# First attention tile with one Newton step for all heads, weights converted one slot ahead of use, and earlier weight splits

## The chip, the cores and the metric

The kernel runs on one NeuronCore of a Trainium2 chip. The engines that matter are TensorE (PE, matrix products), VectorE (DVE), ScalarE (ACT), GpSimd (POOL) and SyncE (SP, which issues most transfers). The metric is the device time of one execution in microseconds, as the median of the runs shown. A profile comes from one of those executions, with times counted from its first instruction.

## The reference

Linear attention of 8 batches, 8 heads, 576 positions and head width 64, with a normalisation, then a two-layer network with a rational activation on 4608 tokens (512 to 2048 to 512), all in float32:

```python
kv = np.einsum('bhsd,bhse->bhde', k, v)
out = np.einsum('bhsd,bhde->bhse', q, kv)
rms = np.sqrt(np.mean(out * out, axis=-1, keepdims=True) + 1e-06)
x = out / rms * g_norm   # heads side by side: 4608 x 512
h = x @ w_in
P = a[0] + a[1] * h + a[2] * h**2 + a[3] * h**3
Q = 1.0 + np.abs(b[0]) * np.abs(h) + np.abs(b[1]) * h**2
out = (P / (Q + 1e-06)) @ w_out
```

The two weight matrices arrive as 64-bit floats; their bits are passed in as 64-bit integers and turned into float32 on the chip.

## The kernel before, in words

**Tiles and slots.** The 4608 tokens are nine tiles of 512. The hidden width is 16 chunks of 128. The work runs in 9 x 16 slots (t, c): a slot takes the product of the first layer for one chunk (`gemm1`, h), the activation (`ew_a` to `ew_d`: L423 to L447 on ScalarE and VectorE, giving g), and the second layer's product (`gemm2`) into four accumulators. In slot i, TensorE's order is gemm2 of slot i - 2, a piece of the attention of the next tile, then gemm1 of slot i + 1 (in the first four slots gemm1 stands ahead of the attention). The order of each engine's queue is the order of the code from L569 on; nothing is rearranged there. h has two buffers.

**Precision.** A tile after the first splits every float32 operand into a high and a low part of the type fp32r and takes three products (low by high, high by low, high by high: L413 to L415, L474 to L476). In the first tile the weights are used whole, in one float32 product (L409, L470), since they aren't split yet.

**Weights.** They come as 16 units, eight of `wi` and eight of `wo`, each of two chunks. A unit is fetched by SyncE (`fetch_w`, L156, 1 MB), then its two 32-bit words are scaled on ScalarE (`conv_a`, L172), put together on VectorE (`conv_b`, L189, L194, L195), and later split (`split_w`): a copy to fp32r (L216), and the difference from it on VectorE (L223). The table `schedule` (L120) gives for each unit the slots in which it is fetched, scaled, put together and split, which engine takes what (S for ScalarE, G for GpSimd), and where in the slot the two halves of `conv_b` stand. In this version each split stands in the slot before the unit's first use in tile 1, the copy of the `wo` units is GpSimd's, and units are put together two to three slots ahead of use in tile 0, except the last ones.

**Attention.** For tile t + 1 it is spread over the slots of tile t: K·V of a pair of heads (`att_kv`, L297) in even slots, the product with q (`att_o`) in odd ones, then the mean squares of all heads in one accumulator (`att_ms`), one reciprocal root by ScalarE's Ln and Exp with a Newton step on VectorE (`newton_rstd`, L246 to L252), a spread of that row over partitions through DRAM, and the normalisation (`att_norm`, L376). For tile 1 both are whole float32 products, and the K·V copies stand in `split_kv` (L234, L240, L241).

**The first tile's attention** (L529 to L578) has nothing to hide behind. It takes K·V, o, squares, mean squares, Newton step and normalisation one pair at a time: the mean squares are taken with a matrix `own` that gives every partition its own head's mean at once, so that each pair has its own Ln, Exp, Square (L246 to L248), its own two Newton operations (L251, L252) and its normalisation (L565). Between them stand the two halves of the first unit's conversion ("a0 b0 a1 b1" in `order`, L575).

Of the kernel before, what the change touches and what calls it, by code (L numbers as in the profile page):

```python
# [23 lines left out]
def linear_attention_then_rational_ffn(  # L24
# [51 lines left out]

    ZSC = 2.0**-40
# [25 lines left out]
    zero = work.tile([P, P], F32, tag="at", name="zero", bufs=4)  # L103
    POOL.memset(zero, 0.0)
    for i in range(NKV):
        DVE.tensor_copy(kvh[i], zero)
        DVE.tensor_copy(kvl[i], zero)


    kvf = wpool.tile([P, 2, NPAIR, P], F32, tag=f"f{NF - 1}", name="kvf")  # L110
    POOL.memset(kvf, 0.0)

    def f32(t):
# [5 lines left out]

    schedule = {  # L120
# [16 lines left out]
    }  # L137
    units = list(schedule)
# [11 lines left out]
    def fetch_w(u):  # L150
        kind, c = u
        k = units.index(u) % NG
        raws[u] = wpool.tile([P, 2 * DM], I64, tag=f"g{k}", name=f"raw_{kind}{c}")
        src = w_in[c:c + 2].rearrange("c p k f -> p c (k f)") if kind == "wi" else \
            w_out[c:c + 2].rearrange("c p f -> p c f")
        nc.sync.dma_start(raws[u].rearrange("p (c f) -> p c f", c=2), src)  # L156
# [9 lines left out]
    both = slice(0, 2 * DM)  # L166
# [7 lines left out]
    copy = {"S": ACT.copy, "V": DVE.tensor_copy, "G": POOL.tensor_copy}  # L174

    def conv_a(u, part=both):
        low, high = words(u, part)
        engines = schedule[u][4]
        scale(engines[0], f32(high), f32(high), 2.0**-112)
        scale(engines[1], low, low.bitcast(U32), 2.0**-29)  # L180
# [25 lines left out]
    def split_w(u):  # L206
# [9 lines left out]
        copy[schedule[u][4][2]](wh, w)  # L216
# [220 lines left out]
    def ew_c(t, c, fill=lambda k: None):  # L437
# [5 lines left out]
        if t == 0:  # L443
# [17 lines left out]
    def gemm2(t, c, subs=range(NSUB)):  # L461
# [4 lines left out]
        for k, s in enumerate(subs):  # L466
            ss = slice(k * P, (k + 1) * P)
            o = acc[t][s]
            if t == 0:
# [59 lines left out]
    o0, ms0 = {}, {}  # L529

    def first_kv(p):
        ps = ps_at.tile([P, TW], F32, tag=("at", "ms")[p % 2], name=f"kvp_0_{p}", bufs=1)
# [25 lines left out]
    def first_rstd(p):
        r0[p] = work.tile([P, TW], F32, tag="d", name=f"r_0_{p}")
        r2 = work.tile([P, TW], F32, tag="u", name=f"r2_0_{p}")  # L560
        todo[p] = newton_rstd(ms0[p], r0[p], r2)

    def first_norm(p):
        todo[p]()
        DVE.scalar_tensor_tensor(x0[:, p], o0[p], ghalf, r0[p], ALU.mult, ALU.mult)  # L565

    x0 = xpool.tile([P, NPAIR, TW], F32, tag="xB", name="x0")
    warm = ps_h.tile([P, TW], F32, tag="h", name="warm")
    ctx.enter_context(tc.manual_schedule())  # L569
    PE.matmul(warm, own, kvf[:, 1].rearrange("p a b -> p (a b)"), start=True, stop=True)  # L570
    POOL.tensor_scalar(ghalf, gcol, -0.5, None, ALU.mult)
    steps = {"k": first_kv, "o": first_o, "s": first_sq, "m": first_ms, "r": first_rstd, "x": first_norm,
             "a": lambda n: conv_a(units[0], slice(n * DM, (n + 1) * DM)),
             "b": lambda n: conv_b(units[0], slice(n * DM, (n + 1) * DM))}
    order = "k0 k1 o0 o1 s0 m0 k2 k3 s1 m1 o2 o3 r0 r1 " \  # L575
            "x0 s2 s3 a0 m2 x1 b0 a1 b1 m3 r2 r3 x2 x3"
    for step in order.split():
        steps[step[0]](int(step[1]))  # L578
    for u in at_slot(0, -1)[:3]:
        fetch_w(u)  # L580
    fetch_kvq(1, 0)
    for u in at_slot(0, -1)[3:]:
        fetch_w(u)


    for k in (-2, -1):
        for u in at_slot(2, k):
            conv_b(u)
        for u in at_slot(1, k):
            conv_a(u)  # L590
# [76 lines left out]
```

## Time and profile before

| what | value |
|---|---|
| median of three runs | 948.72 us (948.35 to 952.35) |
| profiled execution, its own time | 952.35 us |
| its span, first to last instruction | 950.5 us |
| TensorE busy | 906.5 us, 95% |
| VectorE busy | 814.2 us, 86% |
| ScalarE busy | 684.8 us, 72% |
| GpSimd busy | 13.8 us, 1% |
| moved by the transfers | 63.78 MB |
| mean granted TensorE clock | 0.983 |

A busy share is an average over stages with different limits, and products are pipelined, so that a busy TensorE isn't one at its peak. The profile's views that are shown later: a table of stretches (busy time of each engine in each, the granted clock, the share of the transfer engines and what they moved), the waits (who waited for whom, in total, how often, the longest), groups of instructions by line, and the timeline (start, duration, engine, line, output<-inputs, shapes, and in brackets the idle time before it and what ended that). A line number is that of the code that issued the instruction; line 172 is the scaling helper, line 234 the copy of K·V.

### The profile page before, as it was taken

Reading aid. Unit: us, or ns where it says so; the run is one execution under the profiler, and the core shown is the slowest. Engines: PE = TensorE matmul, PEld = TensorE weight load, DVE = VectorE, ACT = ScalarE, POOL = GpSimd, SP = SyncE. Lnnn points to the kernel's source line nnn. Section 1 sums busy time; section 2 is a strip of 40 time slices with the busy share of each in tenths; the row PEclk is TensorE's granted clock in tenths of the full one; section 3 lists DMA queues with packets and bytes.
Section 4 is the critical chain, followed back from the end, with each engine's and each line's share of the span. In section 5 each row is a group of like instructions: output and inputs, shape, how many; then the busy total and the mean of one; then the engine's idle time right before and its main releaser. Section 6 shows DMA issues by size and latency. Waiting matters only on the chain.

```text
span 950.5 us, 11596 instructions
## 1 busy us (share of the span) xinstructions
PE 906.5 (95%) x4234; PEld 682.3 (72%) x4234; DVE 814.2 (86%) x1275; ACT 684.8 (72%) x1154; POOL 13.8 (1%) x26
## 2 busy tenths in 40 slices
PE   6599997999979999999999999999999999999998
PEld 3244433776758878887888788878887888788886
DVE  4989998798976789878987898879877998898887
ACT  4867765767656777877786778677877697777766
POOL 1000111000000000000000000000000000000000
PEclk9999998999979999999999999999999999999999
DMA  8634400310103210321032113101310110101001
GB/s 318 243 139 188 167 23 1 116 61 12 45 0 117 73 37 9 117 72 33 14 117 66 28 25 117 61 23 35 106 48 12 45 55 23 33 14 45 1 0 45
DMA packets 26935, 63.78 MB, mean 67 GB/s; under 512 B 3264, under 2 KB 5312, under 8 KB 26880
## 3 DMA queue, kind: packets, MB, share of 16 engines
q1 hardware_dynamic: 26432, 63.06, 20.2%
q8 instruction: 33, 0.54, 0.2%
q14 instruction: 22, 0.18, 0.1%
q10 hardware_dynamic: 448, 0.00, 0.0%
HBM read 53.48 MB, written 9.57 MB: 66 GB/s over the span
## 4 chain that ended last, share of the span: by engine, by line
PE 77%; DVE 16%; ACT 4%; issue 2%; DMA 1%; SPq 0%; DVEq 0%; ACTq 0%
PE h L413 12%; PE acc L475 12%; PE acc L476 11%; PE h L414 11%; PE h L415 11%; PE acc L474 11%; PE kvp L297 2%; PE acc L470 2%; DVE u L441 2%; DVE q L425 2%; DVE u L433 1%; DVE q L439 1%; DVE u L427 1%; DVE wow L195 1%; DVE wol L223 1%
## 5 line engine op out<-in xcount | busy, mean ns | idle before, releaser
L423 ACT ACTIVATE d<-h 128x512 f32<-128x512 f32 x143 | 85.6, 599 | 181.1 <-PE h L415 174.1
L475 PE MATMUL acc<-wol,gh 128*128 128x512 f32 x508 | 200.9, 395 | 10.7 <-DVE wol L223 10.7
L413 PE MATMUL h<-x,parts 128*128 128x512 f32 (+1 forms) x516 | 205.6, 398 | 0.0
L415 PE MATMUL h<-x,parts 128*128 128x512 f32 (+1 forms) x516 | 200.5, 389 | 0.0
L425 DVE SCALAR_TENSOR_TENSOR q<-d,b1abs,q 128x512 f32<-128x512 f32 x143 | 107.2, 749 | 94.3 <-ACT q L424 94.2
L414 PE MATMUL h<-x,wil 128*128 128x512 f32 (+1 forms) x452 | 176.0, 389 | 0.0
L476 PE MATMUL acc<-parts,gh 128*128 128x512 f32 x448 | 175.8, 393 | 0.0
L474 PE MATMUL acc<-parts,gl 128*128 128x512 f32 x448 | 175.6, 392 | 0.0
L434 ACT ACTIVATE d<-q,bias 128x512 f32<-128x512 f32 x143 | 105.5, 738 | 34.9 <-DVE q L425 34.0
L475 PEld LDWEIGHTS acc<-wol,gh 128*128 128x128 f32 x508 | 96.7, 190 | 33.7 <-ACT gh L457 5.4
L413 PEld LDWEIGHTS h<-x,parts 128*128 128x128 f32 x516 | 97.4, 189 | 26.2 <-DVE gl L458 5.0
L415 PEld LDWEIGHTS h<-x,parts 128*128 128x128 f32 x516 | 97.2, 188 | 20.7
L426 ACT ACTIVATE u<-h,na 128x512 f32<-128x512 f32 x143 | 111.9, 782 | 0.0
L441 DVE SCALAR_TENSOR_TENSOR u<-u,na,d 128x512 f32<-128x512 f32 x143 | 107.4, 751 | 0.0
L435 ACT ACTIVATE d<-d,bias 128x512 f32<-128x512 f32 x143 | 103.5, 724 | 4.6
L433 DVE SCALAR_TENSOR_TENSOR u<-u,na,h 128x512 f32<-128x512 f32 x143 | 106.1, 742 | 0.1
L439 DVE SCALAR_TENSOR_TENSOR q<-q,d 128x512 f32<-128x512 f32 x143 | 98.5, 689 | 0.5 <-ACT d L435 0.5
L427 DVE TENSOR_TENSOR u<-u,h 128x512 f32<-128x512 f32 x143 | 97.9, 684 | 0.9
L424 ACT ACTIVATE q<-h,ab 128x512 f32<-128x512 f32 x143 | 98.1, 686 | 0.0
L476 PEld LDWEIGHTS acc<-parts,gh 128*128 128x128 f32 x448 | 85.0, 190 | 17.5
L474 PEld LDWEIGHTS acc<-parts,gl 128*128 128x128 f32 x448 | 84.6, 189 | 17.7
L414 PEld LDWEIGHTS h<-x,wil 128*128 128x128 f32 x452 | 85.3, 189 | 15.9
(135 smaller groups left out, 1100.1 us busy)
## 6 DMA issues: line engine op xcount, KB each, us to landing
kvm<-in_kv_dram SPq DMA_DIRECT2D x32, 512.0 KB
raw_wi<-in_w_in_dram SPq DMA_DIRECT2D x8, 1024.0 KB
raw_wo<-in_w_out_dram SPq DMA_DIRECT2D x8, 1024.0 KB
qr<-in_qT_dram SPq DMA_DIRECT2D x32, 256.0 KB
out_dram<-ob SPq DMA_DIRECT2D x16, 512.0 KB
rb<-rd SPq DMA_DIRECT2D x28, 256.0 KB
kve<-in_kv_tail_dram SPq DMA_DIRECT2D x28, 64.0 KB
kvq<-in_qT_dram SPq DMA_DIRECT2D x4, 256.0 KB
```

The costliest lines, as they stand in the source:

```text
L413: PE.matmul(ph, wh, xl, start=(kc == 0), stop=False)
L414: PE.matmul(ph, wl, xh, start=False, stop=False)
L415: PE.matmul(ph, wh, xh, start=False, stop=(kc == NPAIR - 1))
L425: DVE.scalar_tensor_tensor(q, d, b1abs, q, ALU.mult, ALU.add)
L426: ACT.activation(u, ph, AF.Identity, bias=na[:, 2:3], scale=na[:, 3:4])
L427: DVE.tensor_tensor(u, u, ph, ALU.mult)
L433: DVE.scalar_tensor_tensor(u, u, na[:, 1:2], ph, ALU.add, ALU.mult)
L439: DVE.scalar_tensor_tensor(q, q, QEPS, d, ALU.add, ALU.mult)
L441: DVE.scalar_tensor_tensor(u, u, na[:, 0:1], d, ALU.add, ALU.mult)
L474: PE.matmul(o, gl[:, ss], wh, start=(c == 0), stop=False)
L475: PE.matmul(o, gh[:, ss], wl, start=False, stop=False)
L476: PE.matmul(o, gh[:, ss], wh, start=False, stop=(c == NF - 1))
```

## The change

- **First tile's attention.** The mean squares of the four pairs go to one accumulator (through `sel`, as in the later tiles), so that one Ln, Exp, Square and one Newton step serve all eight heads. A matrix `spread` of ones then gives every partition its head's value: one float32 product with 32 rows per pair, after which the normalisation is done in place on `x0`, to which ScalarE has copied o. Squares and copies follow each o at once. Ten small products of zeros (`warm`) are issued ahead of the first K·V and behind it.
- **Start.** The clears of `kvh` and `kvl` move from VectorE to GpSimd. Unit wi 0 is fetched in two transfers; the scaling of its first half is VectorE's. Wi 2 is put together in halves, the last in slot 0. The fetches of wi 2 and wo 0 stand ahead of tile 1's first attention inputs, that of wi 4 behind them.
- **Schedule.** Fetch, scale and put together: each unit is scaled one slot before it is put together, and put together one slot (or two) before its use; wo 14 in slot 14, no longer 15. All copies of the splits are ScalarE's. The splits stand earlier in the second tile, two of them in some slots, except those of wo 12 and wo 14, which move to the third tile (slots 33 and 35).
- **Second tile.** Chunks 12 to 15 of its second layer use the whole weights and whole g, in one float32 product each, like the first tile. The copies of K·V to `kvf` move from VectorE (L240) to ScalarE.

```diff
+    spread = const.tile([P, P], F32, name="spread")
+    POOL.memset(spread, 0.0)
+    quarters = spread.rearrange("(p r) c -> p r c", r=Q4)
+    for p in range(NPAIR):
+        POOL.memset(spread[p * Q4:p * Q4 + 1, 0:D], 1.0)
+    ACT.dma_start(quarters[:, 1, D:P], quarters[:, 0, 0:D])
...
     for i in range(NKV):
-        DVE.tensor_copy(kvh[i], zero)
-        DVE.tensor_copy(kvl[i], zero)
+        POOL.memset(kvh[i].bitcast(F32), 0.0)
+        POOL.memset(kvl[i].bitcast(F32), 0.0)
...
     schedule = {
+        ("wi", 0): (-2, None, None, 14),
+        ("wi", 2): (-2, None, None, 16),
+        ("wo", 0): (-2, 0, 1, 17),
+        ("wi", 4): (-1, 1, 2, 17),
+        ("wo", 2): (-1, 2, 3, 18),
+        ("wi", 6): (-1, 3, 4, 19),
+        ("wo", 4): (0, 4, 5, 19),
+        ("wi", 8): (0, 5, 6, 20),
+        ("wo", 6): (1, 6, 7, 21),
+        ("wi", 10): (2, 7, 8, 21),
+        ("wo", 8): (3, 8, 9, 23),
+        ("wi", 12): (4, 9, 10, 23),
+        ("wo", 10): (5, 10, 11, 24),
+        ("wi", 14): (6, 11, 12, 26),
+        ("wo", 12): (7, 12, 13, 33),
+        ("wo", 14): (8, 13, 14, 35),
     }
+    LATE = 12
...
+    def unsplit(t, c):
+        return t == 0 or t == 1 and c >= LATE
...
-        copy[schedule[u][4][2]](wh, w)
+        ACT.copy(wh, w)
...
             ACT.copy(kvh[n][js, js], ps[js, 0:D])
+            if t == 1:
+                ACT.copy(kvf[js, 1, p, js], ps[js, 0:D])
...
-        if t == 0:
+        if unsplit(t, c):
             g = gs[t, c] = work.tile([P, TW], F32, tag=("gh", "gl")[c % 2], name=f"g_{t}_{c}")
...
-            if t == 0:
+            if unsplit(t, c):
                 PE.matmul(o, g[:, ss], w32["wo", c], start=(c == 0), stop=(c == NF - 1))
...
+    def warm(n):
+        for _ in range(n):
+            PE.matmul(idle[:, 0:P], zero, zero, start=True, stop=True)
...
     def first_o(p):
         o0[p] = ps_acc.tile([P, TW], F32, tag="acc", name=f"op_0_{p}")
         PE.matmul(o0[p], kvf[:, 0, p], ke[p][:, 4 * P:], start=True, stop=True)
+        sq0[p] = work.tile([P, TW], F32, tag=("q", "d")[p % 2], name=f"sq_0_{p}")
         ACT.activation(sq0[p], o0[p], AF.Square)
+        if p < NPAIR - 1:
+            ACT.copy(x0[:, p], o0[p])
...
+        PE.matmul(ms0[p * Q4:(p + 1) * Q4], sel, sq0[p], start=True, stop=True)
...
+    warm(8)
+    first_kv(0)
+    warm(2)
+    first_o(0)
+    first_kv(1)
+    first_o(1)
+    ms0 = ps_at.tile([P, TW], F32, tag="ms", name="ms_0", bufs=1)
+    first_ms(0)
+    first_kv(2)
+    first_o(2)
+    first_ms(1)
+    first_kv(3)
+    first_o(3)
+    first_ms(2)
+    first_ms(3)
+    for u in at_slot(0, -2)[1:]:
         fetch_w(u)
     fetch_kvq(1, 0)
+    for u in at_slot(0, -1):
         fetch_w(u)
...
+    newton = newton_rstd(ms0, r0, r2)
+    ACT.copy(x0[:, NPAIR - 1], o0[NPAIR - 1])
+    conv_a(units[0], one, "V")
+    conv_b(units[0], one)
+    newton()
+    conv_a(units[0], two)
+    conv_a(units[1], one)
+    for p in range(NPAIR):
+        pool, tag, bufs = ((ps_h, "h", 2), (ps_h, "h", 2), (ps_at, "at", 1), (ps_at, "ms", 1))[p]
+        rb = pool.tile([P, TW], F32, tag=tag, name=f"rb_0_{p}", bufs=bufs)
+        ps = slice(p * Q4, (p + 1) * Q4)
+        PE.matmul(rb, spread[ps], r0[ps], start=True, stop=True)
+        DVE.scalar_tensor_tensor(x0[:, p], x0[:, p], ghalf, rb, ALU.mult, ALU.mult)
+    conv_b(units[0], two)
+    conv_a(units[1], two)
+    conv_b(units[1], one)
...
+        if i == 0:
+            rest[0].append(lambda: conv_b(units[1], two))
         for u in at_slot(2, i):
-            rest[schedule[u][5]].append(lambda u=u: conv_b1(u))
-            rest[schedule[u][6]].append(lambda u=u: conv_b2(u))
+            rest[-1].append(lambda u=u: conv_b1(u))
+            rest[0].append(lambda u=u: conv_b2(u))
```

The table before, for comparison, with the same four slots: wi 2 (-1, -2, -1, 16), wo 0 (-1, -1, 1, 17), wi 4 (-1, -1, 0, 18), wo 2 (-1, 1, 2, 19), wi 6 (-1, 2, 3, 20), wo 4 (0, 3, 4, 21), wi 8 (1, 4, 5, 22), wo 6 (2, 5, 6, 23), wi 10 (3, 6, 7, 24), wo 8 (4, 7, 8, 25), wi 12 (5, 8, 9, 26), wo 10 (6, 9, 10, 27), wi 14 (7, 10, 11, 28), wo 12 (8, 11, 13, 29), wo 14 (9, 14, 15, 31).

More of the change, by code (lines that the diff above doesn't have):

```diff
@@ L75, in linear_attention_then_rational_ffn @@
     ghalf = const.tile([P, 1], F32, name="ghalf")
+    zero = work.tile([P, P], F32, tag="at", name="zero", bufs=4)
+    POOL.memset(zero, 0.0)
+    kvf = wpool.tile([P, 2, NPAIR, P], F32, tag=f"f{NF - 1}", name="kvf")
+    POOL.memset(kvf, 0.0)
     ZSC = 2.0**-40
@@ L155, in fetch_w @@
             w_out[c:c + 2].rearrange("c p f -> p c f")
-        nc.sync.dma_start(raws[u].rearrange("p (c f) -> p c f", c=2), src)
+        to = raws[u].rearrange("p (c f) -> p c f", c=2)
+        for js in ((slice(0, 1), slice(1, 2)) if u == units[0] else (slice(0, 2),)):
+            nc.sync.dma_start(to[:, js], src[:, js])
     def words(u, part):
@@ L164, in words @@
         return w[:, :, 0], w[:, :, 1]
-    both = slice(0, 2 * DM)
+    both, one, two = slice(0, 2 * DM), slice(0, DM), slice(DM, 2 * DM)
     def scale(engine, to, of, by):
@@ L172, in scale, with conv_a @@
             ACT.activation(to, of, AF.Copy, scale=by)
-    copy = {"S": ACT.copy, "V": DVE.tensor_copy, "G": POOL.tensor_copy}
-    def conv_a(u, part=both):
+    def conv_a(u, part=both, engine="S"):
         low, high = words(u, part)
-        engines = schedule[u][4]
-        scale(engines[0], f32(high), f32(high), 2.0**-112)
-        scale(engines[1], low, low.bitcast(U32), 2.0**-29)
+        scale(engine, f32(high), f32(high), 2.0**-112)
+        scale(engine, low, low.bitcast(U32), 2.0**-29)
     def conv_b1(u, part=both):
@@ L526, in linear_attention_then_rational_ffn @@
     fetch_w(units[0])
-    o0, ms0 = {}, {}
+    o0, sq0 = {}, {}
+    def warm(n):
+        for _ in range(n):
+            PE.matmul(idle[:, 0:P], zero, zero, start=True, stop=True)
     def first_kv(p):
-        ps = ps_at.tile([P, TW], F32, tag=("at", "ms")[p % 2], name=f"kvp_0_{p}", bufs=1)
+        pool, tag, bufs = ((ps_at, "at", 1), (ps_h, "h", 2), (ps_h, "h", 2), (ps_at, "at", 1))[p]
+        ps = pool.tile([P, TW], F32, tag=tag, name=f"kvp_0_{p}", bufs=bufs)
         for c in range(5):
@@ L558, in first_rstd @@
[L558 to L565, printed above, removed]
+        PE.matmul(ms0[p * Q4:(p + 1) * Q4], sel, sq0[p], start=True, stop=True)
     x0 = xpool.tile([P, NPAIR, TW], F32, tag="xB", name="x0")
-    warm = ps_h.tile([P, TW], F32, tag="h", name="warm")
+    idle = ps_at.tile([P, TW], F32, tag="ms", name="idle", bufs=1)
@@ L569, in linear_attention_then_rational_ffn @@
     ctx.enter_context(tc.manual_schedule())
-    PE.matmul(warm, own, kvf[:, 1].rearrange("p a b -> p (a b)"), start=True, stop=True)
+    warm(8)
     POOL.tensor_scalar(ghalf, gcol, -0.5, None, ALU.mult)
[L572 to L576, printed above, removed]
@@ L577, in linear_attention_then_rational_ffn @@
-    for step in order.split():
-        steps[step[0]](int(step[1]))
-    for u in at_slot(0, -1)[:3]:
+    first_kv(0)
[13 more added lines that the diff above has]
+    for u in at_slot(0, -2)[1:]:
         fetch_w(u)
     fetch_kvq(1, 0)
-    for u in at_slot(0, -1)[3:]:
+    for u in at_slot(0, -1):
@@ L583, in linear_attention_then_rational_ffn @@
         fetch_w(u)
[L586 to L590, printed above, removed]
+    r0 = work.tile([P, TW], F32, tag="u", name="r_0")
+    r2 = work.tile([P, TW], F32, tag="u", name="r2_0")
+    newton = newton_rstd(ms0, r0, r2)
[11 more added lines that the diff above has]
+        DVE.scalar_tensor_tensor(x0[:, p], x0[:, p], ghalf, rb, ALU.mult, ALU.mult)
```

16 lines of the change are left out of this document (removed), and 16 rows, old and new, of the table schedule.

## The prediction, made before the result was known

> **What bounds the kernel now.** I read the stretches first, cut where the work changes: the start, the first tile's slots, the change to the second tile, the second tile, one later tile, the rest.
>
> ```profile
> core 0: us, PE busy (x) PEld busy (x) DVE busy (x) ACT busy (x) POOL busy (x), PEclk, DMA share, GB/s
> 24.00:48.80 24.80, 13.49 (x49) 5.50 (x49) 23.03 (x34) 20.34 (x30) 0.00 (x0) 0.92 0.67 250
> 48.80:136.60 87.80, 87.80 (x264) 39.52 (x265) 81.78 (x113) 62.99 (x91) 7.01 (x5) 0.98 0.36 134
> 136.60:168.40 31.80, 23.76 (x55) 10.54 (x53) 27.40 (x37) 17.59 (x26) 2.79 (x2) 0.89 0.00 1
> 168.40:287.40 119.00, 105.92 (x493) 81.56 (x492) 101.69 (x150) 78.71 (x133) 1.34 (x1) 0.93 0.16 47
> 287.40:383.30 95.90, 95.90 (x497) 77.92 (x496) 80.02 (x129) 70.50 (x124) 0.00 (x0) 1.00 0.19 58
> 383.30:950.50 567.20, 563.20 (x2785) 459.31 (x2784) 489.98 (x786) 423.82 (x735) 0.00 (x0) 1.00 0.16 48
> ```
>
> From 287.4 us on TensorE is never free: nothing but less TensorE work helps there, and the change takes none away. From 48.8 to 136.6 it is busy throughout too. All that can be won lies before 48.8, from 136.6 to 168.4, and in the second tile, which takes 119.0 us where the next tile takes 95.9. So the waits of TensorE come next, first those from 24 to 170, then those of the second tile.
>
> ```profile
> PE acc L470 <- DVE wow L195: 11.3, 3, 5.4
> PE h L414 <- DVE parts L223: 2.1, 1, 2.1
> ...
> PE acc L475 <- DVE wol L223: 10.7, 7, 2.7
> PE acc L474 <- POOL woh L216: 2.3, 1, 2.3
> ```
>
> Every one ends with a piece of weight preparation: the integer add of a conversion (L195) or a split (L223, L216). The waits have a second price, the clock.
>
> ```profile
> 48.80 5.12 PE L470 MATMUL acc<-wow,g 128*128 128x512 f32 x8 [5.43 <-DVE wow L195]
> ...
> 66.10 3.60 PE L470 MATMUL acc<-wow,g 128*128 128x512 f32 x8
> ...
> 161.81 6.63 PE L470 MATMUL acc<-wow,g 128*128 128x512 f32 x8 [3.87 <-DVE wow L195]
> 168.37 0.69 PE L297 MATMUL kvp<-kvm 128*64 128x64 f32 x16
> ...
> 287.42 0.69 PE L297 MATMUL kvp<-kvm 128*64 128x64 f32 x16
> ```
>
> The same eight passes take 3.60 us, but 5.12 and 6.63 after idle times of 5.43 and 3.87 us: 1.5 and 3.0 us lost to a lower clock. In the second tile the clock averages 0.93, so 0.07 x 119 = 8.3 us went that way; with 10.7 + 2.3 of waits this explains 21.3 of the 23.1 us by which that tile is longer than the next.
>
> **The price of one slot.** One slot of the first tile, VectorE first, then what the other engines do in it:
>
> ```profile
> 115.67 0.74 DVE L425 SCALAR_TENSOR_TENSOR q<-d,b1abs,q 128x512 f32<-128x512 f32 x1
> ...
> 116.93 0.70 DVE L189 TENSOR_SCALAR wow<-raw_wo 128x1024 int32<-128x1024 int32 x1
> ...
> 118.19 0.69 DVE L439 SCALAR_TENSOR_TENSOR q<-q,d 128x512 f32<-128x512 f32 x1
> 118.79 1.22 DVE L194 SCALAR_TENSOR_TENSOR wow<-raw_wo,wow 128x1024 int32<-128x1024 int32 x1
> 120.05 1.23 DVE L195 CUSTOM_DVE_ANT_0 wow<-raw_wo,wow 128x2048 uint16<-128x2048 uint16 x1
> ...
> 121.97 1.41 DVE L447 SCALAR_TENSOR_TENSOR g<-q,u 128x512 f32<-128x512 f32 x1
> 123.31 0.74 DVE L376 SCALAR_TENSOR_TENSOR xf<-xf,ghalf,rb_qh 128x512 f32<-128x512 f32 x1
> 123.97 0.74 DVE L425 SCALAR_TENSOR_TENSOR q<-d,b1abs,q 128x512 f32<-128x512 f32 x1
> ```
>
> ```profile
> 116.03 3.60 PE L409 MATMUL h<-x,wiw 128*128 128x512 f32 x8
> 119.46 3.60 PE L470 MATMUL acc<-wow,g 128*128 128x512 f32 x8
> 119.92 0.58 ACT L423 ACTIVATE d<-h 128x512 f32<-128x512 f32 x1
> 120.39 0.69 ACT L424 ACTIVATE q<-h,ab 128x512 f32<-128x512 f32 x1
> 121.50 1.34 POOL L216 CAST parts<-wow 128x1024 fp32r<-128x1024 f32 x1 [6.29 <-DVE wow L195]
> ```
>
> VectorE needs 123.97 - 115.67 = 8.30 us. Of that 0.74 is a normalisation, and 0.72 is L447 stretched from 0.69 to 1.41 while GpSimd copies weights (121.50). Without both a slot is 6.85, of which the conversion is 0.70 + 1.22 + 1.23 = 3.15. TensorE needs 2 x 3.43 (116.03 to 119.46) = 6.87, and up to 7.8 where attention stands in the slot. After h is done (119.46) ScalarE needs until 121.08, 1.6 us, before VectorE can begin (L425); I call VectorE's start behind TensorE's slot start its lag, 1.5 to 1.6 at best.
>
> **The change, stage by stage.** (1) Up to the first second-layer product, 48.80 now.
>
> ```profile
> 10.00:20.00 10.00, 9.41 (x54) 4.35 (x52) 3.60 (x10) 5.43 (x9) 0.00 (x0) 1.00 1.03 380
> ...
> 8.55 1.12 PE L538 MATMUL kvp<-kvm 128*64 128x64 f32 x16 [1.82 <-DMA kvm<-in_kv_dram]
> 17.54 1.88 PE L545 MATMUL op<-kvq,kvf 128*128 128x512 f32 x4
> ...
> 22.93 0.69 ACT L246 ACTIVATE r<-ms,bias 128x512 f32<-128x512 f32 x1
> 24.41 0.63 ACT L248 ACTIVATE r<-r 128x512 f32<-128x512 f32 x1
> ...
> 21.99 0.42 DVE L189 TENSOR_SCALAR wiw<-raw_wi 128x512 int32<-128x512 int32 x1
> 23.89 0.42 DVE L189 TENSOR_SCALAR wiw<-raw_wi 128x512 int32<-128x512 int32 x1
> 34.33 0.75 DVE L425 SCALAR_TENSOR_TENSOR q<-d,b1abs,q 128x512 f32<-128x512 f32 x1 [1.02 <-ACT q L424]
> ```
>
> Transfers are saturated (share 1.03, 380 GB/s). The second pair's keys are in at 8.55; 2.03 MB follow to the end of the fourth pair, 5.3 us at that rate, 6 at a lower one: about 14.3. From there a chain: products and K·V copies to about 17 (an o is half of 1.88), square and mean to 18.8 to 19.8, then one Ln, Exp, Square (22.93 to 25.04, 2.1) to about 21.5, two Newton steps of VectorE (about 1.4 by L439) to 22.9. Before, four such trios stood on ScalarE and eight steps on VectorE; 3 x 2.1 and 6 x 0.69 go. New are four copies of about 0.6 on ScalarE (under the transfers) and four spread products: no row shows one with 32 rows. They cost 0.86 each (an o) one after the other, nothing after the first if they overlap; I take them in turn, nearest to the o rows, with the normalisations (0.74) behind each. TensorE has then idled some 3.5 us, near the 3.87 that cost the clock, so I add 1.7, half of what four such products at half clock would add. Normalised about 27.5; then the second half of unit wi 0 and the first of wi 2, 1.9 each (21.99 to 23.89), put the first L425 at about 32 against 34.33: bounds 30 (full clock, spread products side by side) and 33.5 (half clock through the chain).
>
> Costed at nothing in this stage, with what hides it: the twelve clears that move from VectorE to GpSimd, the ten warming products and the small spread transfer on ScalarE's queue lie before the first keys or have until 22 to land. The first half of wi 0 is now wholly VectorE's, two scalings of 0.42 to 0.69 (L189 and L439 as bounds) and 1.9: it lands about 1.5 us after the last pair and is done by 19, while VectorE waits for the trio until 21.5; without that cover it costs 3.0. On SyncE's queue wi 0 goes as two transfers, the first attention inputs of tile 1 pass ahead of wi 4 (1.05 MB, 2.8 us at 380 GB/s), and wo 4 and wi 8 pass ahead of its second pair: wi 4 is in by about 27 and scaled in slot 1, near 38; the second pair is read near 52. Behind that pair's q, which waits for the o of slot 1, stands the fetch of wo 6, first touched in slot 6. Nothing is late there; if it were, one transfer of 2.8.
>
> Slot 0 on VectorE is then 3.7 + 1.9 (other half of wi 2) + about 0.5 for two small K·V differences = 6.1; slot 1 carries wo 0, ready 5.6 into it (115.67 to 120.05 + 1.23): 32 + 6.1 + 5.6 = 43.7, say 44, against 48.80: **4.8 us won** (bounds 3 and 7). Wi 4, now in slot 2 instead of slot 0, is what leaves VectorE's path here. From there to the third such product it was 66.10 - 48.80 = 17.3, TensorE's own work and 1.5 of clock; TensorE idles about 3.6 us ahead of it again, so I keep 17.3.
>
> (2) Conversions one slot ahead, up to 168.37. By rows, 11.3 - 5.4 = 5.9 of waits on L195, 2.1 on L223 and 3.0 of clock: 11.0 us are lost. GpSimd's seven copies go (up to 0.72 each on L447), the K·V copies move to ScalarE, and wo 14 is converted in slot 14, not 15, which ends the 3.87 wait. Where the new order can wait: a wo unit is ready at lag + 5.6 in the slot before its use, and TensorE comes for it when that slot's own work is done. In attention slots 1.6 + 5.6 = 7.2 is under 7.8: nothing. In slots 9, 11 and 13, of 6.87 and with Newton and normalisations (0.74) about them, the lag is near 1.9, so 1.9 + 5.6 - 6.87 = 0.6 each, 1.9 together. Slot 14 holds the last conversion, a split (1.22, the row below) and four halves of x (0.69 by L439): 3.7 + 3.15 + 1.22 + 2.8 = 10.9 against 6.87. With a lag of 2.5 the low half of wi 0 is there 9.4 into it, and the first product of tile 1 comes for it after 6.87 + 3.43: 11.9 - 10.3 = 1.6 of waiting. 3.5 remain (bounds 0 and 8): **7.5 us won**.
>
> (3) The second tile, 168.37 to 287.42.
>
> ```profile
> L223 DVE TENSOR_TENSOR wol<-wow,parts 128x1024 fp32r<-128x1024 f32 x7 | 8.5, 1218 | 0.0
> ...
> 345.14 0.39 PE L413 MATMUL h<-x,parts 128*128 128x512 f32 x1
> ...
> 347.86 0.39 PE L474 MATMUL acc<-parts,gl 128*128 128x512 f32 x1
> ```
>
> A group of 12 split products is 347.86 - 345.14 = 2.72, one of 8 whole passes 3.43. Four groups left whole cost 4 x 0.71 = 2.8 (one falls just behind 287.42). VectorE loses two splits (2 x 1.22), the spare copy (0.7) and four gl (0.69): 101.7 - 5.9 = 95.8. ScalarE gains six copies (1.2, twice the 0.58 of a 512-wide pass) and loses four gh of about 0.6: 78.7 + 7.0 - 2.4 = 83. TensorE needs 95.9 + 0.7 (the last whole product of tile 0) + 2.8 = 99.4, and is now the largest. Splits come one to four slots ahead of use instead of one, so a late VectorE no longer holds the product. The lag that may not be passed is about 4.5 in attention slots (6.4 less 1.9 until gl is there). Slot 17 has two copies and the four evacuations on ScalarE (2.4), the lag goes to 3; each slot with two splits (3.7 + 0.7 + 2.4 = 6.8 against 6.3) adds 0.5 and the slot between gives some back: 4.3 at most. That clears by little, so I leave 1.5 of waits (bounds 0 and 10): 119.05 - 100.9 = **18.1 us won**. The two late splits (slots 33, 35) fall under a TensorE that is full, with VectorE 80 of 95.9 busy: nothing; without that cover 2 x 1.2.
>
> Sum: 4.8 + 7.5 + 18.1 = 30.4. The profiled execution took 952.35 (span 950.5), so it becomes 922. It is the longest of the three; the median is 3.6 lower. Whether that difference sits in a stretch that goes I can't see, so I take most of it: **919 us**.
>
> **Rivals.** A: the clock holds through both idle times of the start and the small waits vanish: 919 - 1.7 - 1.5 - 2 = 914. For it: gaps near 2 us (L414's 2.1) did no such harm; against it, 3.87 did. The Trainium skill (TensorE: Matmul & The Clock Gate, Part 1: The HAM clock gate) says that the clock halves after an idle window of about 3.4 us that runs freely; the trace agrees at 3.87 and 5.43, and by that rule gaps of 3.5 us lie at the edge.
>
> B: in slots 17 to 23 VectorE passes that lag, and TensorE waits for gl in five of them by about 2 us: 919 + 10 = 929. For it: ScalarE and VectorE are both near full there; against: they recover in slots 22 to 24.
>
> C: the start wins nothing, the spread and the cold clock taking the place of the Newton steps: 919 + 4.8 = 924. This is also the case that the one Newton step does not do what it says.
>
> D, the other side: conversions one slot ahead reach TensorE late every time. Each of 14 units then costs up to its 3.15 block: 44 us, 963. It decides from 29.7 / 14 = 2.1 us per unit, a lag of 2.2 + 2.1 = 4.3 in every attention slot; against it stands 1.6.
>
> **Chances.** Forecast 0.47, A 0.18, B 0.17, C 0.12, D 0.04, 0.02 for several together near no change. What can be told from no change is 0.5%, 4.7 us. Faster 0.94, same 0.02, slower 0.04. The range takes the bounds of A and B: 909 to 932.
>
> **What would show it.** Right: first L425 near 32; first second-layer product near 44; no wait on L195 above 1 us from slot 4 on; no GpSimd cast; tile 1 near 101 us with waits on wol gone. Wrong: waits for gl or gh in slots 18 to 23; L195 waits in most slots; a TensorE not full in tile 2.

## The result and the profile after

The changed kernel takes 925.48 us (median of four runs, 925.14 to 927.07) against 949.0 us before (four runs, 948.35 to 952.35): a ratio of 0.975, 95% interval 0.972 to 0.977, or 23.5 us won where 30 were forecast. Its profiled execution took 925.14 us, with a span of 923.0.

The stretches of the changed kernel. The cuts at 45.41, 157.84 and 258.95 are the events at which before was cut too (first product of the second layer, change to the second tile, its end), the others are times near those of before; the columns are as before:

```profile
24.00:45.41 21.41, 16.10 (x56) 6.53 (x53) 18.11 (x29) 14.53 (x26) 0.00 (x0) 0.82 0.86 329
45.41:126.00 80.59, 79.82 (x242) 35.50 (x243) 73.12 (x101) 61.16 (x93) 0.00 (x0) 0.97 0.36 133
126.00:157.84 31.84, 29.97 (x76) 13.70 (x74) 31.28 (x44) 20.83 (x31) 0.00 (x0) 1.00 0.05 13
157.84:258.95 101.11, 100.29 (x481) 74.93 (x480) 97.09 (x145) 84.95 (x138) 0.00 (x0) 1.00 0.19 56
258.95:355.00 96.05, 96.05 (x492) 77.05 (x492) 83.67 (x135) 72.63 (x127) 0.00 (x0) 1.00 0.19 58
355.00:923.00 568.00, 563.73 (x2787) 459.67 (x2785) 490.55 (x787) 424.23 (x735) 0.00 (x0) 1.00 0.16 47
```

The second tile went from 119.0 to 101.1 us at full clock; GpSimd is at zero; and from 258.95 on nothing is new. What is left of a lower clock lies early: 0.82 in the first row, 0.97 in the second. The waits of TensorE up to 170 us, in total, how often, the longest:

```profile
PE acc L474 <- DVE wow L199: 5.9, 4, 4.5
PE rb L600 <- DVE r L256: 3.7, 1, 3.7
PE h L418 <- DVE parts L227: 1.2, 1, 1.2
...
PE acc L479 <- DVE wol L227: 0.7, 1, 0.7
```

Before, the conversions (then L195) cost 11.3 in three waits; 4.5 of the 5.9 that remain stand ahead of the first product, and the other three add up to 1.4. The 3.7 is the new idle time ahead of the spread products. In the second tile itself one wait of 0.7 is left of 10.7 + 2.3. The timeline of the changed kernel at the events that the forecast named:

```profile
23.63 2.17 PE L600 MATMUL rb<-r,spread 32*128 32x512 f32 x8 [3.74 <-DVE r L256]
26.59 8.65 PE L413 MATMUL h<-x,wiw 128*128 128x512 f32 x16 [0.80 <-DVE x L601]
...
33.06 0.75 DVE L429 SCALAR_TENSOR_TENSOR q<-d,b1abs,q 128x512 f32<-128x512 f32 x1 [0.76 <-ACT q L428]
...
45.41 6.05 PE L474 MATMUL acc<-wow,g 128*128 128x512 f32 x8 [4.52 <-DVE wow L199]
...
110.61 3.70 PE L474 MATMUL acc<-wow,g 128*128 128x512 f32 x8 [0.30 <-DVE wow L199]
...
157.84 0.69 PE L301 MATMUL kvp<-kvm 128*64 128x64 f32 x16
```

And the clock, by three rows cut around the start's two idle times:

```profile
19.90:30.00 10.10, 5.57 (x13) 2.19 (x14) 5.42 (x9) 5.83 (x10) 0.00 (x0) 0.66 1.03 387
30.00:45.40 15.40, 10.89 (x45) 4.74 (x43) 14.06 (x23) 12.70 (x22) 0.00 (x0) 0.93 0.79 302
45.40:51.40 6.00, 5.99 (x9) 2.67 (x10) 5.93 (x9) 4.79 (x6) 0.00 (x0) 0.60 0.49 199
```

The clock is halved twice (cut to single microseconds, the column reads 1.00 or 0.50, and a value between only where it changes): 0.34 x 10.10 / 0.5 = 6.9 us at half speed around the spread products, and (0.07 x 15.40 + 0.40 x 6.00) / 0.5 = 7.0 us around the first product of the second layer. Sixteen passes of L413, 7.2 at two times 3.60, take 8.65, and eight of L474 take 6.05 instead of 3.60.

Stage by stage, in us of the profiled executions (the second row is from the first to the third product of the second layer; the marker of before is the same event):

| stretch | before | after | won | forecast |
|---|---|---|---|---|
| up to the first second-layer product | 48.80 | 45.41 | 3.4 | 4.8 |
| from it to the third | 17.30 | 18.24 | -0.9 | 0 |
| from there to the second tile | 102.27 | 94.19 | 8.1 | 7.5 |
| second tile | 119.06 | 101.11 | 17.9 | 18.1 |
| rest | 663.06 | 664.09 | -1.0 | 0 |

The sum is 27.5, of 30.4.

### The profile page after: what moved, and what is told of

It is laid out like the page before. It is cut to its first block, busy times and chain, and to the rows that moved or that the text cites. A ratio compares the mean times of both kernels' runs of the same rounds, so it can differ in the third digit from the quotient of the medians.

```text
span 923.0 us, 11585 instructions
## 1 busy us (share of the span) xinstructions
PE 902.8 (98%) x4244; PEld 676.8 (73%) x4244; DVE 799.5 (87%) x1250; ACT 687.6 (74%) x1161; POOL 4.5 (0%) x32
## 4 chain that ended last, share of the span: by engine, by line
PE 83%; DVE 11%; ACT 3%; issue 1%; DMA 1%; SPq 0%; DVEq 0%; ACTq 0%
PE h L417 13%; PE h L418 12%; PE h L419 12%; PE acc L478 11%; PE acc L479 11%; PE acc L480 11%; PE acc L474 4%; PE kvp L301 2%; PE h L413 2%; DVE q L429 1%; DVE q L443 1%; DVE u L445 1%; PE ms L345 1%; ACT parts L220 1%; PE op L332 1%
## 5 line engine op out<-in xcount | busy, mean ns | idle before, releaser
L427 ACT ACTIVATE d<-h 128x512 f32<-128x512 f32 x143 | 85.8, 600 | 166.2 <-PE h L419 149.7
L479 PE MATMUL acc<-wol,gh 128*128 128x512 f32 x492 | 191.8, 390 | 0.7 <-DVE wol L227 0.7
L429 DVE SCALAR_TENSOR_TENSOR q<-d,b1abs,q 128x512 f32<-128x512 f32 x143 | 107.2, 750 | 86.0 <-ACT q L428 85.8
L478 PE MATMUL acc<-parts,gl 128*128 128x512 f32 x440 | 171.7, 390 | 0.0
L480 PE MATMUL acc<-parts,gh 128*128 128x512 f32 x440 | 171.3, 389 | 0.0
L479 PEld LDWEIGHTS acc<-wol,gh 128*128 128x128 f32 x492 | 92.4, 188 | 20.0 <-DVE wol L227 1.0
L478 PEld LDWEIGHTS acc<-parts,gl 128*128 128x128 f32 x440 | 82.6, 188 | 18.2 <-DVE gl L462 0.9
L480 PEld LDWEIGHTS acc<-parts,gh 128*128 128x128 f32 x440 | 82.6, 188 | 17.1
```

The lines of the kernel that those rows point to most:

```text
L429: DVE.scalar_tensor_tensor(q, d, b1abs, q, ALU.mult, ALU.add)
L478: PE.matmul(o, gl[:, ss], wh, start=(c == 0), stop=False)
L479: PE.matmul(o, gh[:, ss], wl, start=False, stop=False)
L480: PE.matmul(o, gh[:, ss], wh, start=False, stop=(c == NF - 1))
```

## The experiments

Three theories were at stake. One: the new first attention is worth what its step said. Two: the gain is the place of the weight work, conversions and splits each. Three: what the start fell short by is the clock. Every edit below is to the changed kernel. The first four were timed beside the kernel before and not beside the changed one, whose median was 925.48 us in the first timing and 926.25 in a later one, so that a difference of 1 us in medians says nothing there.

**The old first attention under the new schedule.** The four Ln/Exp trios, eight Newton operations and `own` come back. With them the ten products of zeros go, ScalarE scales all of wi 0 again, and wi 2 is put together whole ahead of slot 0, so that slot 0 has no conversion; all else of the change stays.

```diff
-    newton = newton_rstd(ms0, r0, r2)
...
-        PE.matmul(rb, spread[ps], r0[ps], start=True, stop=True)
...
+    order = "k0 k1 o0 o1 s0 m0 k2 k3 s1 m1 o2 o3 r0 r1 " \
+            "x0 s2 s3 a0 m2 x1 b0 a1 b1 m3 r2 r3 x2 x3"
...
+    conv_a(units[1])
+    conv_b(units[1])
...
-            rest[0].append(lambda: conv_b(units[1], two))
```

> The changed kernel with the first tile's attention of before (one Ln, Exp, Square and one Newton step per pair, mean squares through the matrix own); wi 2 put together whole ahead of slot 0; all else as changed. Theory S (the start was won by the conversions that left slot 0 and by the scalings of wo 0 and wi 4 that no longer stand ahead of the first activation on ScalarE): the first L429 comes near 33.3 as in the changed kernel (33.06), slot 0 has 1.9 us less on VectorE, and the time is 0 to 2 us below the changed kernel, about 924. Rival N (the single Newton step with the spread won it): the first L429 goes back to 35 or later and the time is 3 us or more above, 928.5 or more.

It took 923.38 us (921.05 to 924.28), ratio 0.972 (0.970 to 0.974): not slower than the change. The profile is of the fastest of its four executions (921.05). Its start on TensorE's timeline, from the first first-layer product on:

```profile
22.75 1.98 PE L411 MATMUL h<-x,wiw 128*128 128x512 f32 x4 [1.67 <-DVE wiw L197]
26.76 1.13 PE L411 MATMUL h<-x,wiw 128*128 128x512 f32 x2 [2.02 <-DVE x L567]
28.87 6.14 PE L411 MATMUL h<-x,wiw 128*128 128x512 f32 x10 [0.98 <-DVE x L567]
...
44.09 3.70 PE L472 MATMUL acc<-wow,g 128*128 128x512 f32 x8 [3.59 <-DVE wow L197]
```

The old attention lets the first product begin pair by pair, so its idle times are 1.67, 2.02 and 0.98, not one of 3.74. The clock still drops there, but less (ten passes in 6.14, where the pace of 3.60 for eight gives 4.5), and the first second-layer product stands at 44.09 and runs at full speed (3.70). The third comes at 59.97, against 63.65 after and 66.10 before. VectorE's first L427 (L429 of the changed kernel) stands at 32.19, where rival N had 35 or later. So the one Newton step with its spread won nothing here; what the start gained over before, it gained elsewhere in the change.

**Conversions back in their old slots.** Only the slots of scaling and putting together go back; splits, copies and the new first attention stay.

```diff
-        ("wo", 0): (-2, 0, 1, 17),
-        ("wi", 4): (-1, 1, 2, 17),
-        ("wo", 2): (-1, 2, 3, 18),
+        ("wo", 0): (-2, -1, 1, 17),
+        ("wi", 4): (-1, -1, 0, 17),
+        ("wo", 2): (-1, 1, 2, 18),
...
-        ("wo", 14): (8, 13, 14, 35),
+        ("wo", 14): (8, 14, 15, 35),
...
+    for u in at_slot(1, -1):
+        conv_a(u)
```

> The changed kernel with units scaled and put together in the slots of before (wi 4 in slot 0, each unit two to three slots ahead of use, wo 14 in slot 15), with the new first attention and the new splits. Theory S: VectorE's slot 0 is 3.15 us longer, so that the first second-layer product comes 3 us later, and the wait on wo 14 with its clock drop at the end of tile 0 comes back for some 5 us: 8 us slower (5 to 12), 933. Rival N (the Newton step and the clock made the difference, the slots of the conversions none): within 2 us of 925.5.

932.36 us (931.12 to 934.04), ratio 0.982 (0.980 to 0.984). TensorE's waits up to 170 us:

```profile
PE acc L474 <- DVE wow L199: 8.4, 2, 4.5
...
PE op L327 <- DVE kvl L245: 2.5, 1, 2.5
PE h L418 <- DVE parts L227: 1.5, 1, 1.5
```

The wait ahead of the last `wo` unit is back (8.4 - 4.5 = 3.9, as before), and so is the clock drop behind it: from the third second-layer product to the second tile it takes 99.45, 5.2 more than the change's 94.19. The first second-layer product stands at 50.75, 5.3 later than in the first profile of the change, but 2.6 later than in its second (48.13, shown below with the products of zeros), and by the third product 1.4 of that is left (68.44 against 67.08). So the slots of the conversions are worth some 6.6 us, of which 5.2 lie behind the third product. The other 2.8 us by which that stretch was longer before (102.27 against 99.45) were not tried alone.

**Splits just in time.** Eleven splits go back to the slot before their use; the last two stay in the third tile.

```diff
-        ("wi", 4): (-1, 1, 2, 17),
-        ("wo", 2): (-1, 2, 3, 18),
+        ("wi", 4): (-1, 1, 2, 18),
+        ("wo", 2): (-1, 2, 3, 19),
...
-        ("wi", 14): (6, 11, 12, 26),
+        ("wi", 14): (6, 11, 12, 28),
```

> The changed kernel with the splits of all units but wo 12 and wo 14 put back to the slots of before, each in the slot ahead of its use; the amount of work is the same. Theory P (position: TensorE waited for the low half of a wo unit that was split one slot ahead): waits on wol of 1 to 2 us come back in every second slot from 20 to 28, with a clock drop near the end; second tile 7 us longer (5 to 12), 932. Rival W (amount: the tile was won by the operations taken out of VectorE, two splits, a copy and four gl): 0 to 2 us, at most 927.5.

932.68 us (932.33 to 933.19), ratio 0.982 (0.980 to 0.984). Its second tile as a stretch, and TensorE's one line of waits in it:

```profile
159.68:267.18 107.50, 100.87 (x482) 74.83 (x481) 97.47 (x145) 84.46 (x138) 0.00 (x0) 1.00 0.17 52
```

```profile
PE acc L479 <- DVE wol L227: 6.6, 6, 2.0
```

VectorE's work is the same (97.5 against 97.1); only the place of it differs, and the tile is 6.4 us longer: 6.6 of waits in place of 0.7, all on the low half of a `wo` unit. The clock drop that theory P expected did not come: with these waits the clock stays at 1.00.

**All units split in the second tile.** Nothing is left whole there.

```diff
-        ("wo", 12): (7, 12, 13, 33),
-        ("wo", 14): (8, 13, 14, 35),
+        ("wo", 12): (7, 12, 13, 28),
+        ("wo", 14): (8, 13, 14, 30),
...
-    LATE = 12
+    LATE = 16
```

> The changed kernel with wo 12 and wo 14 split in slots 28 and 30 of the second tile and no chunk of that tile left whole. TensorE has 2.8 us less, VectorE 5.9 us more (two splits of 1.22, a copy of 0.7, four gl of 0.69). Theory V (in the last slots of that tile VectorE would be the later one): x of the third tile comes late in slot 31, TensorE waits there some 4 us; 2 to 5 us slower than the changed kernel, about 929. Rival T (TensorE sets that tile): 2.8 us faster, 922.7.

927.15 us (926.99 to 928.77), ratio 0.977 (0.975 to 0.979). The second tile as a stretch, and TensorE's waits in it:

```profile
158.04:261.82 103.78, 99.83 (x493) 76.65 (x492) 99.48 (x149) 87.21 (x142) 0.00 (x0) 1.00 0.18 54
```

```profile
PE h L417 <- DVE x L268: 2.3, 3, 1.4
PE acc L478 <- DVE gl L462: 0.8, 1, 0.8
PE acc L479 <- DVE wol L227: 0.7, 1, 0.7
```

The tile is 2.7 longer, though TensorE's work in it falls by 0.5: VectorE is 2.4 busier, and products now wait for x (2.3 us in three waits, where theory V had some 4) and gl (0.8). Behind the tile 0.7 comes back, the whole product that no longer falls there. The direction is that of theory V. The size (1.7 in the medians) is within the intervals of the two ratios.

**GpSimd's copies.** The `wo` copies go back to GpSimd.

```diff
-        ACT.copy(wh, w)
+        (POOL.tensor_copy if kind == "wo" else ACT.copy)(wh, w)
```

> The changed kernel with the fp32r copies of the wo units given back to GpSimd. Theory G (a GpSimd copy stretches the VectorE operation beside it by 0.7): six of them run early, in slots 8 to 14 of the first tile, where VectorE has nothing to spare; 2 to 4 us slower, 928.5, with L451 of 1.3 to 1.4 in the first tile. Rival H (the stretch is hidden and ScalarE is relieved): within 1 us.

929.51 us (928.25 to 931.76), ratio 0.980 (0.978 to 0.982), 3.3 more than the changed kernel beside it (926.25). The activation's last operation, as a group of instructions from 60 to 158 us (count, busy us, mean ns of one, idle time before), first in the changed kernel:

```profile
L451 DVE SCALAR_TENSOR_TENSOR g<-q,u 128x512 f32<-128x512 f32 x13 | 9.0, 691 | 1.0
```

and with GpSimd's copies:

```profile
L451 DVE SCALAR_TENSOR_TENSOR g<-q,u 128x512 f32<-128x512 f32 x12 | 12.3, 1023 | 1.0
```

Its stretches from the third second-layer product to the second tile, and the second tile:

```profile
63.85:164.18 100.33, 92.94 (x262) 41.80 (x261) 96.03 (x125) 72.24 (x107) 9.76 (x7) 0.98 0.25 93
164.18:263.43 99.25, 99.25 (x482) 75.21 (x481) 95.85 (x144) 78.16 (x131) 0.00 (x0) 1.00 0.18 56
```

The mean goes from 691 to 1023 ns: six of these operations, each beside a cast on GpSimd, take 1.33 to 1.41 us (1.3 to 1.4 expected), the others 0.69. That is some 4 us. The first tile loses 6.1 us (100.33 against 94.19); the second gains 1.9, with ScalarE busy 78.2 of it and not 85.0 and TensorE never free. The Trainium skill (SBUF — State Buffer, Who interferes with whom) says that a VectorE instruction with two SBUF inputs contends with a GpSimd instruction that reads SBUF, over a port pair that it calls an exclusive lock; the trace agrees, with 0.64 to 0.72 us more for each of the six.

**Products of zeros in the two idle times.** Nothing of the computation changes.

```diff
     first_ms(3)
+    warm(14, ps_h.tile([P, TW], F32, tag="h", name="idle_1"))
...
+        if i == LAG:
+            warm(18, ps_at.tile([P, TW], F32, tag="ms", name="idle_2", bufs=1))
```

> The changed kernel with 14 and 18 small products of zeros added in TensorE's two idle times of the start, ahead of the first spread product and ahead of the first second-layer product; nothing else is changed. Theory K (the idle times cost the clock): no drop to half clock near 23 and 43 us, the first second-layer product takes 3.6 and not 5.9; 2 to 4 us faster than the changed kernel, 922.3. Rival D (VectorE's chain sets the start, the clock is hidden under it): within 1 us.

The changed kernel was timed again beside it.

> The changed kernel itself, beside the next three on one chip: 925.5, within 1.5.

921.05 us (920.78 to 922.39), ratio 0.971 (0.969 to 0.973), against 926.25 (925.38 to 928.41), ratio 0.976 (0.974 to 0.978), for the changed kernel on the same chip: 5.2 us from 32 products of zeros. On the timeline, first with the products of zeros:

```profile
19.92 3.39 PE L537 MATMUL idle<-zero 128*128 128x128 f32 x28
23.73 1.26 PE L601 MATMUL rb<-r,spread 32*128 32x512 f32 x8 [0.42 <-DVE r L256]
...
43.72 3.70 PE L474 MATMUL acc<-wow,g 128*128 128x512 f32 x8 [0.50 <-DVE wow L199]
```

then the changed kernel again, without:

```profile
24.92 2.17 PE L600 MATMUL rb<-r,spread 32*128 32x512 f32 x8 [3.74 <-DVE r L256]
27.89 10.08 PE L413 MATMUL h<-x,wiw 128*128 128x512 f32 x16 [0.80 <-DVE x L601]
...
48.13 6.76 PE L474 MATMUL acc<-wow,g 128*128 128x512 f32 x8 [4.52 <-DVE wow L199]
```

The idle time ahead of the spread products is the same 3.74 as in the first profile, and yet sixteen passes take 10.08 here and 8.65 there. So the same idle time costs one of several amounts. Of the 3.4 us by which the two profiles of one kernel differ in span (926.4 and 923.0), 1.3 lie ahead of the spread products (24.92 against 23.63), 1.4 in these passes and 0.7 in the eight of L474. The 1.3 go with the clock too: the first pair's product with q takes 1.91 us in the second profile (at 7.75) and 1.10 in the first (at 7.07), as the first products of the program run at half speed for longer there (the clock column reads 1.00 up to the first change that the trace recorded, at 9.96 and 5.80). With the gaps filled, whose spread products start at 23.73 like those of the first profile, the third second-layer product comes at 59.61, 4.0 before that profile's and 0.4 before the old attention's, and the clock doesn't drop:

```profile
19.90:30.00 10.10, 8.75 (x46) 5.39 (x46) 6.23 (x11) 6.37 (x12) 0.00 (x0) 1.00 1.03 397
```

The Trainium skill (TensorE: Matmul & The Clock Gate, Part 1: The HAM clock gate) has the activity watched in free-running windows of some 3.4 us, so that a loss depends on where in the window an idle time falls; the two profiles agree. In both the clock changes only at whole multiples of 3.41 us from its first drop (at 22.87, 29.69, 43.35 and 50.17 in the first). Cut into such windows (the columns are those of the stretches, with TensorE's busy time first), the first profile shows

```profile
19.45:22.87 3.42, 0.44 (x2) 0.00 (x0) 0.89 (x3) 2.87 (x5) 0.00 (x0) 1.00 1.02 401
22.87:26.28 3.41, 2.17 (x8) 0.62 (x8) 1.10 (x2) 2.96 (x6) 0.00 (x0) 0.50 1.04 351
26.28:29.69 3.41, 3.10 (x4) 1.51 (x5) 3.27 (x6) 0.00 (x0) 0.00 (x0) 0.50 1.03 412
```

the second

```profile
20.20:23.61 3.41, 0.98 (x3) 0.07 (x2) 0.91 (x2) 2.33 (x4) 0.00 (x0) 1.00 1.03 387
23.61:27.03 3.42, 2.11 (x8) 0.62 (x8) 1.13 (x2) 3.42 (x7) 0.00 (x0) 0.50 1.04 384
27.03:30.44 3.41, 2.61 (x4) 1.17 (x4) 3.32 (x6) 0.08 (x1) 0.00 (x0) 0.50 1.02 408
30.44:33.85 3.41, 3.41 (x5) 1.33 (x4) 2.85 (x5) 0.00 (x0) 0.00 (x0) 0.50 1.03 412
```

and the old attention

```profile
25.27:28.68 3.41, 1.13 (x2) 0.30 (x2) 3.31 (x5) 2.52 (x3) 0.00 (x0) 1.00 1.03 410
...
38.92:42.33 3.41, 1.57 (x6) 0.60 (x4) 3.38 (x6) 3.23 (x5) 0.00 (x0) 1.00 0.23 43
42.33:45.75 3.42, 1.66 (x4) 0.87 (x5) 3.35 (x5) 2.97 (x6) 0.00 (x0) 1.00 1.03 401
```

The clock is halved behind windows in which TensorE was busy for 0.44, 0.98 and 1.13 us, and holds behind 1.57 and 1.66, over which the idle time of 3.59 is spread. It comes back behind the first window that is busy nearly throughout (3.10 and 3.41), not behind 2.17, 2.11 or 2.61. So the first profile pays two windows at half speed and the second three, for the same idle time.

**Conversions into the idle times.** The first fill stays. Instead of the second, wi 0, wi 2 and the scaling of wo 0 stand ahead of slot 0, wo 0 is put together in slot 0, and split in slot 16.

```diff
-        ("wo", 0): (-2, 0, 1, 17),
+        ("wo", 0): (-2, None, 0, 16),
...
+    conv_a(units[0], two, "V")
+    conv_b(units[0], two)
     newton()
-    conv_a(units[0], two)
     conv_a(units[1], one)
+    conv_b(units[1], one)
+    conv_a(units[1], two)
+    conv_a(units[2])
...
-    conv_b(units[0], two)
-    conv_a(units[1], two)
-    conv_b(units[1], one)
+    conv_b(units[1], two)
```

> The changed kernel with the products of zeros ahead of the first spread product, and VectorE's idle times of the start filled: both halves of wi 0 put together while ScalarE has Ln, Exp and Square, the first half of wi 2 while the spread products run, the second ahead of slot 0, wo 0 scaled before slot 0 and put together in it, and split in slot 16. Theory S: the first L429 comes near 31, VectorE's slots 0 and 1 are 1.9 and 3.15 shorter in front of the first second-layer product, which comes near 39, not 45.4; 6 to 9 us faster than the changed kernel, 918. Rival E (something else then stands there, the transfers or TensorE): 0 to 3 us.

922.27 us (920.66 to 922.34), ratio 0.971 (0.970 to 0.973): 4.0 under the changed kernel on the same chip, not 6 to 9, and not below the kernel with the products of zeros (921.05).

```profile
39.50 3.60 PE L474 MATMUL acc<-wow,g 128*128 128x512 f32 x8
...
58.02 5.40 PE L474 MATMUL acc<-wow,g 128*128 128x512 f32 x8 [2.57 <-DVE wow L199]
```

The first product stands at 39.50 with no wait, 5.9 earlier than after, as hoped, and 4.2 earlier than with the products of zeros (43.72). But the third comes at 58.02 only, 2.57 behind a conversion that had stayed where it was, and that wait brings a clock drop (5.40 for 3.60). The gap was moved, not closed. The second tile is 1.2 longer too (102.35), which I put down to the split in slot 16; that was not tried alone.

**All conversions one slot earlier.** As the last, with each later unit scaled and put together a slot earlier and wo 0 split in slot 17 again.

```diff
-        ("wo", 0): (-2, None, 0, 16),
-        ("wi", 4): (-1, 1, 2, 17),
-        ("wo", 2): (-1, 2, 3, 18),
+        ("wo", 0): (-2, None, 0, 17),
+        ("wi", 4): (-1, 0, 1, 17),
+        ("wo", 2): (-1, 1, 2, 18),
...
-        ("wo", 14): (8, 13, 14, 35),
+        ("wo", 14): (8, 12, 13, 35),
```

> The kernel of the run with the gaps of the start used, with every later unit also put together one slot earlier (wi 4 in slot 1, wo 2 in slot 2 and so on to wo 14 in slot 13) and wo 0 split in slot 17 again. Theory L (in that run the 4 us won in front of the first second-layer product were lost at wo 2, which was still put together in slot 3): no wait on L199 above 0.5 us after the first second-layer product, the third one near 55.3 and not 58.0, the waits of slots 10, 12 and 14 (0.3 to 0.7 each) gone too; 916, 5 to 6 us below the run with products in the idle times (921.05). Rival M (VectorE's sum over the first slots sets it whatever the order): the third one stays near 58 or later, 920 to 922.

916.7 us (915.49 to 918.73), ratio 0.9645 (0.9624 to 0.9667).

```profile
24.00:40.75 16.75, 14.39 (x60) 6.52 (x59) 15.13 (x24) 12.10 (x21) 0.00 (x0) 1.00 0.89 349
40.75:149.75 109.00, 106.82 (x317) 48.32 (x316) 106.03 (x147) 84.09 (x128) 0.00 (x0) 1.00 0.31 113
149.75:250.80 101.05, 100.28 (x481) 74.90 (x480) 97.04 (x145) 84.94 (x138) 0.00 (x0) 1.00 0.18 56
```

No stretch shows a lower clock, and no wait on L199 is left; the third second-layer product stands at 56.53 (55.3 expected). From the first second-layer product to the second tile it takes 109.0 against 112.4 after, and that product stands 4.7 earlier: 8.1 us less up to the second tile, which is as long as it was. This is a version that beats both kernels, by 34 us the one before on the same chip.

**And wi 0 split early.** As the last, with the first unit's split in slot 7.

```diff
-        ("wi", 0): (-2, None, None, 14),
+        ("wi", 0): (-2, None, None, 7),
```

> The same with the split of wi 0 in slot 7, not 14. Theory: the wait of TensorE on the low half of wi 0 at the end of the first tile (1.2 us, L418) goes; 1 us faster than the run beside it. Rival (slot 7 has no room on VectorE): the same or up to 1 us slower.

915.76 us (914.48 to 917.79), ratio 0.9639 (0.9615 to 0.9662), which can't be told from the last. In the trace the aim was met, the wait of the first `wi` product for that split (1.7 us) is gone; from the third second-layer product to the second tile it takes 91.73 instead of 93.22. The second tile gives 0.6 of this back (101.69).

**Before, profiled again.** The kernel before, unchanged, to find where its profiled execution was longer than its median.

> The kernel before itself, a second profile of it: where its executions differ (948.35 to 952.35). Theory C (the clock): the stretches without idle times of TensorE (from the third second-layer product to 136, and from 287 on) last the same to 0.2 us, and the difference lies where the clock drops, at the start or in the second tile. Rival F (transfers or something spread out): stretches differ everywhere.

It took 949.34 us, with a span of 947.5, 3.0 less than the profile that the forecast was made from. The second tile of this execution:

```profile
167.74:284.42 116.68, 103.58 (x493) 79.96 (x492) 101.69 (x150) 78.72 (x133) 1.34 (x1) 0.96 0.16 48
```

It has the same work on VectorE as the first profile's (101.69), but a clock of 0.96, not 0.93, and is 2.4 us shorter. The start is 0.9 shorter (first second-layer product at 47.92); the stretches between and behind agree to 0.1 or 0.2. So 2.4 us of the longer execution were clock drops in the second tile, behind waits that the change takes away; the 0.9 at the start go with the clock too. They have arisen by the third pair's K·V (14.82 in the first profile, 13.96 here), and the first two pairs' products with q, four passes, take 3.78 us there and 3.16 here: half speed for longer at the start of the program.

## Why the prediction was nearly right

**What bounds it** held: all of the gain lies ahead of 258.95, and the rest of the kernel is 1.0 slower, 0.7 of it in the third tile (96.58 up to 355.53, where before had 95.89): the one whole product that the prediction had seen there, counted within its 2.8. "Every one ends with a piece of weight preparation" holds for the waits that it shows; ahead of 48.80, 5.8 us of others ended with the first attention, the activation or a K·V difference.

**The start** was expected to have its first L425 (now L429) at 32 and its first second-layer product at 44; they came at 33.06 and 45.41, inside the bounds, but at 35.78 and 48.13, outside them, in the second profile: that the first one fits is luck in part. From L429 to that product it took 12.35, where 6.1 + 5.6 = 11.7 had been summed. The spread products were costed in turn at 0.86 each, 3.4 for four. They overlap: four take 1.26 us at full clock and 2.17 in the changed kernel. The Trainium skill (TensorE: Matmul & The Clock Gate, Part 3: Packing small matmuls) measured 3.07 times for four products of 32 rows on different rows of the array; the trace agrees in kind, with 4 x 0.86 / 1.26 = 2.7. What was saved there the clock took: the idle time was 3.74 (3.5 expected), and half speed cost 0.9 in the spread products and 1.45 in the first-layer ones, where I had added 1.7 in all; and the chain ahead was late, with the spread at 23.63 and in the second profile at 24.92, where Newton was to end at 22.9. The step that reads "I keep 17.3" was mis-sized in the same way: the idle time ahead of the first second-layer product was 4.52, not 3.6, and its eight passes took 6.05, not 5.12 (which they had taken behind 5.43 of idle time: length alone doesn't set the loss). Together these are 2.3 us of the 2.9 by which the sum fell short; the later stretches nearly cancel, +0.6, -0.2 and -1.0.

**Conversions one slot ahead** won 8.1 (7.5 expected). Waits of 0.6 each were worked out for three slots; there are three, of 1.4 together. The 1.6 on the low half of wi 0 was 1.2. **The second tile** was 101.11, expected 100.9, but by two errors that cancel: 1.5 of waits were allowed and 0.7 seen, while TensorE was busy for 100.29, where 99.4 had been summed; no run shows where that 0.9 goes. The two experiments on it show that the place of the splits (6.4 us) counts for more than the two left out of it (2.7). The other 8.8 of the 17.9 won there were not tried alone; in the profile of before, by the prediction's own sum, 8.3 were the clock.

**Rivals.** A (the clock holds) is not what the change does, but what it lacks: with the gaps filled the medians differ by 5.2 and the profiles by 4.0, where A had 1.7 + 1.5 for the clock and 2 for small waits, which stayed. B (waits for gl in slots 17 to 23) and D (every conversion late) didn't happen. C (the start wins nothing) fell for the start as a whole, which won 2.5 by the third product in the first profile (63.65 against 66.10); in the second it is 1.0 behind (67.08). Its time, 924, is the nearest of all, and its second half is true: by the first experiment the Newton step and the spread don't make the start shorter. The prediction put that start's gain on the attention chain and the conversions at once and could not part them. Its test for the clock, the length of one idle time ("gaps near 2 us did no such harm"), is not the one that the runs bear out: 2.02 and 0.98 close together cost the clock, 2.57 did, and 3.59 spread over two windows didn't. For the ends of its range, 909 and 932, it shows no sum.

**The step that failed most** is "I take most of it": 3.0 us taken off, because the profiled execution of before was 3.6 above the median. This excess doesn't carry over: by the second profile of before, 2.4 of it lay in clock drops of the second tile, which the change clears anyway, and 0.9 in the clock of the start. In part it was thus taken off twice. The changed kernel's profiled execution is within 0.4 of its median (925.14, 925.48). Of the 6.5 us by which 919 is too low, 3.3 are this and 3.2 the sum (the 2.9, and 0.3 of what lies around the span).

## What to carry to other kernels

Where preparation is made just in time, its place counts before its amount: the same splits a slot or two earlier were worth 6.4 us, and a conversion moved out of one gap (4.2 us won at the first product) is worth little until the next unit in the chain moves as well. Idle time on TensorE has a second price, the clock, so a restructured chain that works less but leaves one long gap may win nothing over a longer one with short gaps; products of zeros in the gap tell the two apart, and may stay. What counts in these traces is how busy TensorE is in each stretch of 3.41 us, not the length of one gap. When a profiled execution is longer than the median, look where the excess sits before taking it off the forecast.

## What was not expected of the hardware

The same kernel with the same 3.74 us of idle time lost 1.4 us more (8.65 against 10.08 for sixteen passes) in one execution than in another, one window of 3.41 us more at half speed, and 3.59 us of idle time, with the old attention, lost nothing (3.70 for eight passes). Four float32 products of 32 rows by 512, on different rows of the array, took 1.26 us together, where four of 128 rows take 3.43. And 28 small passes of zeros (128 by 128, 3.39 us) were enough to hold the clock at 1.00.
